# Moving the parts of an attention head by a slot in a hand-planned schedule

## The chip, the cores and the metric

The kernel runs on one core of a Trainium2 chip. The metric is the device time of one execution in microseconds (us), as a median over several executions; lower is better.

## The reference

Attention with a causal window of 128 and ALiBi slopes (4 batches, 8 heads, 576 positions, head size 64), and two layers that each multiply the 2304 rows by a 512x2048 and a 2048x512 matrix:

```python
scores = scale * np.matmul(q, k.transpose(0, 1, 3, 2))
mask = (rel >= 0) & (rel < 128)
scores = np.where(mask, scores + bias[None], -1000000000.0)
attn = np.exp(scores - np.max(scores, axis=-1, keepdims=True))
attn = attn / (np.sum(attn, axis=-1, keepdims=True) + 1e-09)
x = heads_side_by_side(np.matmul(attn, v))          # 2304 x 512
...
h = x @ w_in;  g = h * np.clip(h + 3.0, 0.0, 6.0) / 6.0;  x = g @ w_out     # first layer
h = x @ w_in;  g = s * np.maximum(h, 0.0) ** 2 + b;       x = g @ w_out     # second layer
```

## The kernel before

**Groups, heads, steps.** The rows are cut into eight groups of one batch each: four of 256 rows (two 128-row blocks), then four of 320 rows (three blocks, of which the last has 64 rows). Attention of group g makes the tile x of group g, in eight heads. The heads of groups 0 and 1 have a form of their own (class StartUnit). From group 2, "the third group", on they are of class Unit, 48 in all. The first layer goes through the groups, in 16 steps f for each: a step multiplies x by one 128-column piece of w_in (the twelve matmuls of h, L576), applies the activation, and multiplies by the piece of w_out (o, L634, twelve matmuls). A step's matmuls have 256 columns in groups 0 to 3 and 320 in groups 4 to 7. The second layer follows in tiles of 384 rows (L648). Each value is split into a rounded part ("hi") and a remainder ("lo"), so that every product is made of three matmuls.

**The order.** All instructions are written down by a planner: `at(slot, rank, fn)` puts a function into a slot, and the program is emitted slot by slot, by rank within one. Each engine executes its instructions in that order. Layer steps are two slots apart, heads four slots apart, so two steps stand beside each head; those whose f is even and odd are called the even and the odd step here. While group g's steps run, the heads of groups g+1 and g+2 are made.

**One step's chain.** h goes to PSUM, in one bank (tag "h", a single buffer) up to the last group. ScalarE (ACT) applies ReLU (L589), VectorE (DVE) multiplies (L593, called the product below) and so frees the bank: the next step's h waits for it. Then ACT rounds (L606) and DVE takes the remainder (L613); o of that step comes after the next step's h.

**One head's chain (Unit).**

- `load` (L277, L283): DMAs on the SP queue, into one of two buffers raw. A load waits until the head two before has been read by its remainders.
- `casts` (L291, L292, ACT): rounded q and k.
- `rests` (L296 on DVE, L301 on GpSimd, POOL): their remainders.
- `products` (L320, PE): scores of the first two blocks ("first products"), and a slot later of the third block ("second products"), which heads of groups 4 to 7 alone have. There are 32 of those heads.
- `minima` (L336, L337, DVE), `exps` (L347, ACT), `sums` (L354, L357, DVE), `weights` (L363, POOL: division by the sum).
- `transposes` (L372, PE), `fold` (L376, ACT: copy to F), `masks` (L388, POOL).
- every second head `values` (L403, PE), `to_hi` (L414, ACT) and `to_lo` (L418, DVE: remainder of x).

Up to about 140 us the weights of the first layer are still being prepared (class Half): a DMA (L168) on the same SP queue, two ACT instructions (L178, L179, tile z), two on DVE (L183, L186), one on POOL (L192), one on ACT (L200) and one on DVE (L204). This part of the time is called the weight stage.

Of the kernel before, what the change touches and what calls it, by code (L numbers as in the profile page):

```python
# [23 lines left out]
def tile_alibi_window_attention_moe_moe2(  # L24
# [45 lines left out]
    def at(slot, rank, fn):  # L70
        plan.setdefault(slot, []).append((rank, len(plan[slot]), fn))
# [70 lines left out]
    class Half:  # L142
# [10 lines left out]
        def plan(self, s):  # L153
            at(s - 3, 1, self.load)
            at(s, 30.1, self.high)
            at(s, 38, self.sign)
            at(s + 1, 31, self.add)
            at(s + 2, 31.2, self.hi)
            at(s + 3, 31, self.lo)
# [79 lines left out]
    class Unit:  # L239
# [10 lines left out]
        def plan(self, s):  # L250
            two = min(self.qa + 2, self.qb)
            at(s - 7, 1, self.load)
            at(s - 1, 34, self.casts)
            at(s + 1, 33, self.rests)
            at(s + 3, 20, lambda: self.products(self.qa, two))
            at(s + 4, 20, lambda: self.products(two, self.qb))
            at(s + 3, 32, lambda: self.minima(self.qa, two))
            at(s + 4, 32.7, lambda: self.minima(two, self.qb))
            at(s + 5, 33, lambda: self.exps(self.qa, two))
            at(s + 5, 33, lambda: self.exps(two, self.qb))  # L260
            at(s + 6, 32.2, self.sums)
            at(s + 7, 33, self.weights)
            at(s + 9, 20, self.transposes)
            at(s + 9, 35, self.fold)
            at(s + 10, 30.02, self.masks)
            if self.h % 2:
                at(s + 13, 20, self.values)
                at(s + 14, 39, self.to_hi)
                at(s + 15, 39, self.to_lo)

        def pair(self):
            return units[self.g * H + self.h // 2 * 2 :][:2]
# [444 lines left out]
    for f in range(NF):  # L717
        for i, s in enumerate((hslot[0, f], oslot[0, f])):
# [3 lines left out]
            s = min(s - 6, 3 + 4 * f + 2 * i)  # L722
# [3 lines left out]
    for k in range(2 * NF):  # L726
        f, i = divmod(k, 2)
        s = max(last + 6 + int(1.74 * k), oslot[nt1 - 1, f])
# [25 lines left out]
    with tc.manual_schedule():  # L754
        for slot in sorted(plan):
            for _, _, fn in sorted(plan[slot], key=lambda x: x[:2]):
                fn()
# [55 lines left out]
```

## Time and profile before

| | us |
|---|---|
| median of 3 executions (953.79 to 955.13) | 953.92 |
| the profiled execution | 956.32 |
| its span, first to last instruction | 954.5 |
| PE busy in the span | 930.8 |
| weight loads of PE (PEld) busy | 857.1 |
| DVE busy | 531.2 |
| ACT busy | 466.2 |
| POOL busy | 271.7 |

The profiled execution is one more execution, 2.4 us over the median; 1.8 us of its time lie outside the span. PE's matmuls and its weight loads are shown as two engines, PE and PEld. The granted clock of TensorE was 0.999 over the whole span.

### The profile page before, as it was taken

How to read it: one execution, taken by the hardware profiler on the slowest of the kernel's cores; microseconds unless marked ns; L12 is line 12 of the kernel's file. 1: busy time of each engine (PE TensorE's matmuls, PEld its weight loads, DVE VectorE, ACT ScalarE, POOL GpSimd, SP SyncE). 2: the span in 40 equal slices, each digit the busy share in tenths (PEclk: the TensorE clock that was granted, in tenths of full speed). 3: DMA queues.
4: the chain of work that ended last, by engine and by line, in shares of the span. 5: the costliest groups of instructions: out<-in, count | busy, mean ns of one | idle time of the engine just before them, and what ended most of it. 6: DMA issues, size and time to landing. Idle time of an engine off the chain costs nothing.

```text
span 954.5 us, 16386 instructions
## 1 busy us (share of the span) xinstructions
PE 930.8 (98%) x6014; PEld 857.1 (90%) x6017; DVE 531.2 (56%) x1334; ACT 466.2 (49%) x1201; POOL 271.7 (28%) x544
## 2 busy tenths in 40 slices
PE   8898999999999999999999999999999999999998
PEld 4587899999999999999999988899999999999997
DVE  6998885555555555555259999633323323323322
ACT  6987875455455454454248757523223223323322
POOL 6635763345544434443114433100000000000000
PEclk9999999999999999999999999999999999999999
DMA  8425533123131222220045355010200200200000
GB/s 319 147 70 177 172 112 99 58 89 96 61 95 61 71 75 62 73 78 13 1 158 192 133 183 163 25 41 1 67 1 1 67 1 1 67 1 1 34 1 33
DMA packets 34383, 73.92 MB, mean 77 GB/s; under 512 B 4352, under 2 KB 13568, under 8 KB 34304
## 3 DMA queue, kind: packets, MB, share of 16 engines
q1 hardware_dynamic: 34304, 72.89, 23.2%
q8 instruction: 47, 0.77, 0.3%
q14 instruction: 32, 0.26, 0.1%
HBM read 63.44 MB, written 9.44 MB: 76 GB/s over the span
## 4 chain that ended last, share of the span: by engine, by line
PE 75%; DVE 13%; ACT 4%; issue 3%; DMA 3%; POOL 1%; SPq 0%; POOLq 0%; ACTq 0%; DVEq 0%
PE h L576 34%; PE o L648 18%; PE o L634 16%; DVE w L204 3%; DVE z L183 3%; PE s L320 3%; PE v L403 3%; DMA raw<-w 2%; PE t L372 2%; DVE raw L186 1%; DVE t L597 1%; ACT z L178 1%; DVE g L613 1%; DVE g L615 1%; DVE t L593 1%
## 5 line engine op out<-in xcount | busy, mean ns | idle before, releaser
L576 PE MATMUL h<-x,w 128*128 128x384 f32 (+2 forms) x2688 | 444.9, 314 | 4.5 <-DVE t L593 3.9
L576 PEld LDWEIGHTS h<-x,w 128*128 128x128 f32 x2688 | 416.4, 189 | 15.6 <-DVE t L593 6.3
L589 ACT ACTIVATE t<-h 128x384 f32<-128x384 f32 (+2 forms) x224 | 99.5, 444 | 366.4 <-PE h L576 366.3
L634 PE MATMUL o<-g,w 128*128 128x256 f32 (+1 forms) x1536 | 230.4, 299 | 2.5 <-ACT g L606 1.2
L648 PE MATMUL o<-w,g 128*128 128x512 f32 x864 | 217.0, 395 | 3.4 <-ACT g L608 1.9
L634 PEld LDWEIGHTS o<-g,w 128*128 128x128 f32 x1536 | 210.0, 189 | 4.7 <-ACT g L606 2.0
L648 PEld LDWEIGHTS o<-w,g 128*128 128x128 f32 x864 | 159.9, 188 | 36.3 <-ACT g L608 4.4
L597 DVE SCALAR_TENSOR_TENSOR t<-t,s_sb 128x384 f32<-128x384 f32 x96 | 63.2, 658 | 171.5 <-ACT t L589 171.5
L388 POOL TENSOR_SCALAR_AFFINE_SELECT W<-F 128x128 f32<-128x128 f32 (+1 forms) x240 | 68.2, 322 | 150.1 <-ACT F L376 149.1
L593 DVE SCALAR_TENSOR_TENSOR t<-t,h 128x256 f32<-128x256 f32 (+1 forms) x128 | 57.6, 450 | 84.1 <-ACT t L589 84.1
L613 DVE TENSOR_TENSOR g<-t,g 128x256 fp32r<-128x256 f32 (+1 forms) x128 | 72.5, 566 | 40.9 <-ACT g L606 40.2
L615 DVE SCALAR_TENSOR_TENSOR g<-t,b_sb,g 128x384 fp32r<-128x384 f32 x96 | 63.6, 663 | 54.1 <-ACT g L608 54.0
L608 ACT ACTIVATE g<-t,b_sb 128x384 fp32r<-128x384 f32 x96 | 59.2, 617 | 63.6 <-DVE t L597 63.6
L192 POOL TENSOR_TENSOR raw<-raw 128x512 int32<-128x512 int32 x47 | 54.9, 1168 | 105.5 <-DVE raw L186 73.1
L606 ACT ACTIVATE g<-t 128x256 fp32r<-128x256 f32 (+1 forms) x128 | 55.9, 436 | 15.5 <-DVE t L593 15.4
L301 POOL TENSOR_TENSOR C<-raw,C 64x448 fp32r<-64x448 f32 (+1 forms) x48 | 51.0, 1063 | 36.2 <-issue 18.4
L363 POOL TENSOR_SCALAR P<-P,st 128x128 f32<-128x128 f32 x128 | 53.2, 431 | 7.1 <-DVE st L357 5.6
L347 ACT ACTIVATE P<-P,st 128x128 f32<-128x128 f32 x128 | 49.6, 391 | 0.0
L336 DVE COPY_PREDICATED s<-own,s 128x128 f32<-128x128 int32 (+1 forms) x112 | 30.8, 275 | 32.4 <-PE s L320 30.7
L183 DVE TENSOR_SCALAR z<-z 128x512 int32<-128x512 int32 x64 | 44.1, 689 | 3.3 <-ACT z L178 2.8
L337 DVE CUSTOM_DVE_ANT_0 P<-s,rel 128x128 f32<-128x128 f32 x128 | 37.1, 290 | 7.3
L204 DVE TENSOR_TENSOR w<-raw,w 128x512 fp32r<-128x512 f32 x47 | 41.2, 876 | 0.0
(73 smaller groups left out, 762.8 us busy)
## 6 DMA issues: line engine op xcount, KB each, us to landing
raw<-w SPq DMA_DIRECT2D x47, 512.0 KB, 4.3
raw<-qk SPq DMA_DIRECT2D x32, 384.0 KB, 3.1
stage<-w SPq DMA_DIRECT2D x17, 512.0 KB, 4.4
out<-y SPq DMA_DIRECT2D x18, 256.0 KB, 2.3
raw<-qk SPq DMA_DIRECT2D x16, 256.0 KB, 2.7
rv<-v SPq DMA_DIRECT2D x16, 256.0 KB, 3.4
raw<-qkv0p SPq DMA_DIRECT2D x8, 384.0 KB, 7.7
x2d<-y SPq DMA_DIRECT2D x8, 320.0 KB, 2.4
```

What stands on the lines that cost most here:

```text
L183: nc.vector.tensor_scalar(out=z, in0=z, scalar1=3, scalar2=None, op0=ALU.logical_shift_left)
L204: nc.vector.tensor_tensor(out=w[:, 1, self.c], in0=self.l.bitcast(F32), in1=w[:, 0, self.c].bitcast(F32), op=ALU.subtract,)
L388: nc.gpsimd.affine_select(out=self.W[:, o : o + r], in_=self.F[:, q : q + r], fill=0.0, base=k - 1, compare_op=ALU.is_ge, pattern=[[s, r]] ...
L576: nc.tensor.matmul(self.ps, lhsT=w[:, wp, cc * P : (cc + 1) * P], rhs=x[:, cc, xp], start=m == 0, stop=m == 3 * CC - 1,)
L589: nc.scalar.activation(self.a, self.ps, AF.Relu, **bias)
L593: nc.vector.scalar_tensor_tensor(out=self.a, in0=self.a, scalar=6.0, in1=self.ps, op0=ALU.min, op1=ALU.mult)
L597: nc.vector.scalar_tensor_tensor(out=self.a, in0=self.a, scalar=s_sb, in1=self.a, op0=ALU.mult, op1=ALU.mult)
L608: nc.scalar.activation(self.g[:, 0], self.a, AF.Identity, bias=b_sb)
L613: nc.vector.tensor_tensor(out=self.g[:, 1], in0=self.a, in1=hi, op=ALU.subtract)
L615: nc.vector.scalar_tensor_tensor(out=self.g[:, 1], in0=self.a, scalar=b_sb, in1=hi, op0=ALU.add, op1=ALU.subtract,)
L634: nc.tensor.matmul(acc[t][d], lhsT=w[:, wp, DM + d * P : DM + (d + 1) * P], rhs=self.g[:, gp], start=f == 0 and i == 0 and (t > 1 or d % 2 ...
L648: nc.tensor.matmul(acc[t][tb], lhsT=self.g[:, gp, tb * P : (tb + 1) * P], rhs=w[:, wp, DM:], start=f == 0 and i == 0, stop=f == NF - 1 and ...
```

## The change

Seven of the numbers that place a head's parts are changed: casts, remainders and division move one slot ahead; transposes, copy, masks, values and the two stores of x one slot back. Loads, products, minima, exponentials and sums stay.

```diff
@@ class Unit, plan @@
             at(s - 7, 1, self.load)
-            at(s - 1, 34, self.casts)
-            at(s + 1, 33, self.rests)
+            at(s - 2, 34, self.casts)
+            at(s, 33, self.rests)
...
-            at(s + 7, 33, self.weights)
-            at(s + 9, 20, self.transposes)
-            at(s + 9, 35, self.fold)
-            at(s + 10, 30.02, self.masks)
+            at(s + 6, 33, self.weights)
+            at(s + 10, 20, self.transposes)
+            at(s + 10, 35, self.fold)
+            at(s + 11, 30.02, self.masks)
             if self.h % 2:
-                at(s + 13, 20, self.values)
-                at(s + 14, 39, self.to_hi)
-                at(s + 15, 39, self.to_lo)
+                at(s + 14, 20, self.values)
+                at(s + 15, 39, self.to_hi)
+                at(s + 16, 39, self.to_lo)
```

What it does to the order is shown at one place that repeats: steps 6 and 7 of group 3, with heads 4 to 7 of group 4 (names s0_2_6 and qY0_102<-raw0_2_7 are the scores of its head 6 and the remainder of q of its head 7; t3_6 and h3_6 are the activation and h of step 6).

On DVE, from the second minima of head 6 to the sums, before:

```order
L336 COPY_PREDICATED s0_2_6_4_3508<-own_90,s0_2_6_4_3508 128x64
L337 ISA P0_2_6_3470,st0_2_6_3471<-s0_2_6_4_3508,rel_91 128x128
L337 ISA st0_2_6_3471 128x1
L593 SCALAR_TENSOR_TENSOR t3_6_3522<-t3_6_3522,h3_6_3495 128x256
L296 SCALAR_TENSOR_TENSOR qY0_102<-raw0_2_7_3291,qX0_98 128x320
L613 TENSOR_TENSOR g3_6_3564<-t3_6_3522,g3_6_3564 128x256
```

and of the change:

```order
L336 COPY_PREDICATED s0_2_6_4_3507<-own_90,s0_2_6_4_3507 128x64
L337 ISA P0_2_6_3475,st0_2_6_3476<-s0_2_6_4_3507,rel_91 128x128
L337 ISA st0_2_6_3476 128x1
L296 SCALAR_TENSOR_TENSOR qY0_102<-raw0_2_7_3293,qX0_98 128x320
L418 TENSOR_TENSOR x4_3251<-v0_2_3_3434,x4_3251 128x320
L593 SCALAR_TENSOR_TENSOR t3_6_3520<-t3_6_3520,h3_6_3494 128x256
L613 TENSOR_TENSOR g3_6_3555<-t3_6_3520,g3_6_3555 128x256
```

The remainder of q, which stood behind step 6's product L593, now stands ahead of it, and so does, at every second head, the remainder of x (L418), which stood two slots further up, ahead of an L613.

On PE, from h of step 6 to the first products of head 7, before (the left out rows are the twelve of o):

```order
L576 MATMUL h3_6_3495<-x3_2383,w1_6_886 128x256 x12
L320 MATMUL s0_2_6_4_3508<-C0_2_6_3361,qX1_99 128x192
L320 MATMUL s0_2_6_4_3508<-C0_2_6_3361,qY1_103 128x192
L372 MATMUL t0_2_5_3518<-ident_89,P0_2_5_3352 128x128 x3
...
L576 MATMUL h3_7_3544<-x3_2383,w1_7_976 128x256 x12
L320 MATMUL s0_2_7_2_3569<-C0_2_7_3479,qX0_98 128x256
```

and of the change:

```order
L576 MATMUL h3_6_3494<-x3_2401,w1_6_886 128x256 x12
L320 MATMUL s0_2_6_4_3507<-C0_2_6_3338,qX1_99 128x192
L320 MATMUL s0_2_6_4_3507<-C0_2_6_3338,qY1_103 128x192
...
L576 MATMUL h3_7_3538<-x3_2401,w1_7_976 128x256 x12
L372 MATMUL t0_2_5_3551<-ident_89,P0_2_5_3358 128x128 x3
L320 MATMUL s0_2_7_2_3568<-C0_2_7_3455,qX0_98 128x256
```

The transposes (and values, where there are any) have moved from between h of the even step and h of the odd step to behind h of the odd step.

On ACT, from the ReLU of step 6 to that of step 7, before:

```order
L589 ACTIVATE t3_6_3522<-h3_6_3495 128x256
L347 ACTIVATE P0_2_6_3470,st0_2_6_3471<-P0_2_6_3470,st0_2_6_3471 128x128 x3
L376 ACTIVATE F0_2_5_3530<-t0_2_5_3518 128x320
L606 ACTIVATE g3_6_3564<-t3_6_3522 128x256
L589 ACTIVATE t3_7_3574<-h3_7_3544 128x256
L291 ACTIVATE qX1_99<-raw1_2_0_3397 128x320
```

and of the change:

```order
L589 ACTIVATE t3_6_3520<-h3_6_3494 128x256
L347 ACTIVATE P0_2_6_3475,st0_2_6_3476<-P0_2_6_3475,st0_2_6_3476 128x128 x3
L606 ACTIVATE g3_6_3555<-t3_6_3520 128x256
L291 ACTIVATE qX1_99<-raw1_2_0_3399 128x320
L292 ACTIVATE C1_2_0_3563<-raw1_2_0_3399 128x448
L376 ACTIVATE F0_2_5_3566<-t0_2_5_3551 128x320
L589 ACTIVATE t3_7_3580<-h3_7_3538 128x256
```

Casts and copy F have come to stand ahead of the odd step's ReLU.

## Rows read from the trace of the kernel before

**Rows 1.** Windows: busy time (and instructions) by stage; clock, DMA share, GB/s.

```profile
core 0: us, PE busy (x) PEld busy (x) DVE busy (x) ACT busy (x) POOL busy (x), PEclk, DMA share, GB/s
60.00:140.00 80.00, 72.72 (x568) 66.93 (x568) 71.71 (x175) 64.26 (x163) 50.38 (x68) 1.00 0.42 137
140.00:475.00 335.00, 335.00 (x2649) 327.12 (x2648) 179.01 (x646) 162.17 (x543) 142.46 (x370) 1.00 0.21 66
```

**Rows 2.** Waits of PE's weight loads, 60 to 140 us: total, times, longest.

```profile
PEld h L576 <- DVE t L593: 5.5, 9, 1.4
```

**Rows 3.** Who waited for the score matmuls L320, whole span: us, times.

```profile
  DVE s L336: 30.7, 32
```

**Rows 4.** Timeline of PE's weight loads at a 256-column step: start, us, what.

```profile
240.27 0.19 PEld L320 LDWEIGHTS s<-C,qX 128*128 128x128 f32 x1
...
240.52 0.32 PEld L372 LDWEIGHTS t<-ident,P 128*128 128x128 f32 x3
240.81 1.50 PEld L634 LDWEIGHTS o<-g,w 128*128 128x128 f32 x12
242.23 0.43 PEld L576 LDWEIGHTS h<-x,w 128*128 128x128 f32 x3
```

**Rows 5.** Timeline of DVE at the same step.

```profile
240.79 0.23 DVE L336 COPY_PREDICATED s<-own,s 128x64 f32<-128x64 int32 x1 [0.61 <-PE s L320]
...
241.27 0.42 DVE L593 SCALAR_TENSOR_TENSOR t<-t,h 128x256 f32<-128x256 f32 x1
241.60 0.48 DVE L296 SCALAR_TENSOR_TENSOR qY<-raw,qX 128x320 fp32r<-128x320 f32 x1
```

**Rows 6.** Timeline of PE's weight loads at a 320-column step.

```profile
303.67 0.19 PEld L320 LDWEIGHTS s<-C,qX 128*128 128x128 f32 x1
...
303.94 0.32 PEld L372 LDWEIGHTS t<-ident,P 128*128 128x128 f32 x3
304.23 1.76 PEld L634 LDWEIGHTS o<-g,w 128*128 128x128 f32 x12
305.95 0.19 PEld L576 LDWEIGHTS h<-x,w 128*128 128x128 f32 x1
```

**Rows 7.** Timeline of DVE at that step.

```profile
304.21 0.23 DVE L336 COPY_PREDICATED s<-own,s 128x64 f32<-128x64 int32 x1 [1.05 <-PE s L320]
...
304.69 0.48 DVE L593 SCALAR_TENSOR_TENSOR t<-t,h 128x320 f32<-128x320 f32 x1
305.09 0.49 DVE L296 SCALAR_TENSOR_TENSOR qY<-raw,qX 128x320 fp32r<-128x320 f32 x1
```

**Rows 8.** Timeline of DVE at a remainder of x.

```profile
239.36 0.49 DVE L418 TENSOR_TENSOR x<-v,x 128x320 fp32r<-128x320 f32 x1
239.76 0.41 DVE L613 TENSOR_TENSOR g<-t,g 128x256 fp32r<-128x256 f32 x1
```

**Rows 9.** Timeline of PE's weight loads where h waits, in the weight stage.

```profile
64.23 1.51 PEld L576 LDWEIGHTS h<-x,w 128*128 128x128 f32 x12
65.67 1.51 PEld L634 LDWEIGHTS o<-g,w 128*128 128x128 f32 x12
67.59 0.30 PEld L576 LDWEIGHTS h<-x,w 128*128 128x128 f32 x2 [0.40 <-DVE t L593]
```

**Rows 10.** The product on DVE that it waited for.

```profile
67.12 0.41 DVE L593 SCALAR_TENSOR_TENSOR t<-t,h 128x256 f32<-128x256 f32 x1
```

**Rows 11.** Timeline of ACT: a ReLU, and a copy F.

```profile
240.64 0.38 ACT L589 ACTIVATE t<-h 128x256 f32<-128x256 f32 x1 [1.84 <-PE h L576]
...
249.26 0.44 ACT L376 ACTIVATE F<-t 128x320 f32<-128x320 f32 x1 [0.33 <-PE t L372]
```

**Rows 12.** Timeline of POOL and DVE: remainder of k, and an L613 beside it.

```profile
245.42 1.16 POOL L301 TENSOR_TENSOR C<-raw,C 64x448 fp32r<-64x448 f32 x1
...
246.12 0.74 DVE L613 TENSOR_TENSOR g<-t,g 128x256 fp32r<-128x256 f32 x1
```

**Rows 13.** Waits of the SP queue, 56 to 145 us: total, times, longest.

```profile
SPq L277 <- DVE qY L296: 70.9, 10, 17.1
```

**Rows 14.** Timeline of ACT: a weight piece that has not landed.

```profile
126.80 0.65 ACT L178 ACTIVATE z<-raw 128x512 f32<-128x512 f32 x1 [0.87 <-DMA raw<-w]
```

**Rows 15.** Waits of DVE, 60 to 140 us: total, times, longest.

```profile
DVE z L183 <- ACT z L178: 2.8, 4, 1.0
```

**Rows 16.** Line L296, all instructions: duration in ns, least, median, greatest.

```profile
L296 DVE SCALAR_TENSOR_TENSOR qY<-raw,qX x48: 409/484/835, 70.8 to 444.7; 128x320 fp32r<-128x320 f32 x32, 128x256 fp32r<-128x256 f32 x16
```

## The prediction

> **What bounds the kernel now.** I read the windows by stage first, then PE's waits, then the timelines of single steps. From 140 to 475 us PE is busy for the whole 335 us [rows 1]: in this stretch nothing but the number of matmuls sets the time, and no other engine is busy for more than 179 us. It holds most of the 48 moved heads, and a move can save nothing there; it can only bring a wait where there is none. In the weight stage, 60 to 140 us, PE is busy for 72.7 of 80 us and DVE for 71.7 [rows 1]. There PE waits above all for the product that frees the bank of h [rows 2]. All that the change may win is there, all that it may lose is after it.
>
> **What the change does from 140 us on: the even step.** DVE waits for the second products before the second minima, at all 32 heads that have them [rows 3]. So that piece of DVE's queue is tied to PE: minima start right behind the score matmuls, then comes the product, and the next h waits for it. The change puts the remainder of q, and at every second head the remainder of x, between the two, and takes the transposes (and values) out of PE's stretch up to that h. DVE's part gets longer and PE's shorter.
>
> A 256-column step, counted from the first load of the second products (240.27 [rows 4]). PE: three transpose loads take 240.52 to 240.81, 0.29; without them o's loads start at 0.25, and h's 1.42 later (240.81 to 242.23), at 1.67. DVE: the product starts at 1.00 (241.27 [rows 5]) and takes 0.42. A 320-wide instruction of the remainder's kind takes its engine 0.40 up to the next one (304.69 to 305.09 [rows 7]), the remainder of x as much (239.36 to 239.76 [rows 8]). With the remainder of q ahead the product ends at 1.82, with both at 2.22. From a product's end to the waiting load were 0.06 us (67.12 + 0.41 to 67.59 [rows 9, 10]), so h's loads start at 1.88 or 2.28: **0.21 or 0.61 late**. That such a wait counts in full is seen in the same rows: from o to h 1.92 instead of 1.44.
>
> A 320-column step, from 303.67 [rows 6]: o at 0.27, h 1.72 later, at 1.99. The product now starts at 1.02 and takes 0.48 [rows 7]; it ends at 1.90 or 2.30, and h is released at 1.96 or 2.36: **0 or 0.37 late**, the first with 0.03 to spare.
>
> How many of each: a head's second products stand 16 slots and 4 for each later head of its group ahead of its group's first step. So heads 0 to 7 of group 4 and 0 to 2 of group 5 have 256-column steps beside them, 11; the other 21 have 320. The remainder of x of an odd head falls three heads later, on heads with an even number: 6 of the 11 and 10 of the 21. Sum: 6 x 0.61 + 5 x 0.21 + 10 x 0.37 + 11 x 0 = **8.4 us**. Bounds: with the full durations, 0.49 in place of 0.40 for each instruction, 0.30, 0.79, 0.06 and 0.55, or 12.4. If one weight load could be made while h waits (1.42/12 or 1.72/12, 0.12 or 0.14 at each of 21 late steps), 5.7. I take 8.4, since rows 9 show the first load of a waiting h not made ahead. The Trainium skill ("TensorE: Matmul & The Clock Gate", the section on the array's architecture) says that PE's queue can pull weight loads ahead of matmuls in flight. By that rule the sum would be near 5.7; the load at 67.59 started only with its release, and the trace decides.
>
> **The odd step.** Its ReLU now stands behind copy F, which waits for the transposes behind h. Until the next h PE has these (0.29), the first products and o (1.42 or more), over 1.71 us; the chain is transposes 0.29, F 0.44, ReLU 0.38 [rows 11], product 0.42, so 1.53. The first products' four loads are the margin; it costs nothing. With that cover gone it would be a few tenths at 32 heads.
>
> L613 of the odd step also comes later by about F's 0.44, and may then run beside POOL's remainder of k, which follows the masks now. In such a meeting it took 0.74 instead of 0.41 [rows 8, 12]. Idle ahead of the second minima were 0.61 (256) and 1.05 (320) [rows 5, 7]; 0.44 + 0.33 is over the former by 0.16. For the 11 heads that is 0 to 1.8; I take half, **0.9**.
>
> Heads without second products (groups 2 and 3, up to about 195 us): remainders stand on DVE in time that is idle, as the product waits for h alone; nothing. Division a slot earlier and transposes a slot later: more slack, and PE did not wait there; nothing. The loads' waits move with the remainders; nothing here, since a load has most of two heads' time to land.
>
> **The weight stage.** Loads of q and k wait on the SP queue for the remainder of the head two before, 70.9 us in ten waits [rows 13]. The weight pieces' DMAs stand behind them on that queue, and a piece was late for ACT by 0.87 [rows 14]. With the remainders a slot ahead these DMAs start earlier. What hangs on it is DVE's wait for z: 2.8 us in four waits [rows 15]. On the other side, F and casts now delay the odd step's ReLU by up to 0.44 at some seven heads, 3.1 at most. The greatest gain is all of DVE's idle time, 80 - 71.7 = 8.3. I take the wait for z, **-2.8**, which is nearest to the cause, and keep +3.1 to -8.3.
>
> **Sum.** 8.4 + 0.9 - 2.8 = 6.5. The profiled execution took 956.32 (span 954.5 and 1.8 around it), so 962.8 for it; the median lies 2.4 lower: 953.92 + 6.5 = **960.4 us**. No change can be told from one within 0.2%, or 1.9 us, here.
>
> **The rivals.** (1) *The weight stage gives more than the steps lose.* If the late pieces were what all engines of that stage hang on, the whole 8.3 comes back, and the steps cost their lower bound, 5.7: 951.3. For it speaks that all ten waits end with the remainder; against it that DVE is 90% busy there and that its own order isn't shortened. It decides from a gain over the steps' loss: a weight stage shorter by 8 us. (2) *They cancel*: a gain of 7 to 8 against 8.4, 953 to 955.5, no difference. (3) *Remainders meet on the shared side.* Both remainders of a head now stand in one slot. If they run at the same time, DVE's takes its longest, 835 ns instead of 484 [rows 16]: 0.35 more at 32 heads, 11 us, so 971. Against it: POOL must first do the masks, which wait for F, while DVE waits for the second products, later. The Trainium skill ("SBUF — State Buffer", the section on two separate sides) says that DVE with two SBUF inputs and a GpSimd instruction that reads SBUF lock each other out for a whole instruction; by that rule a remainder that comes second waits for up to all of the other. Rows 12 agree: L613 ends 0.28 after POOL's instruction.
>
> **How the numbers follow.** My forecast, a wait of h at even steps beside a small gain in the weight stage: 0.70, with 956 to 966 of its own. Rival 3 0.08, rival 2 0.12, rival 1 0.10. The range of 8 in 10 takes in rival 2 and the forecast up to its upper bound: 954 to 967. Slower by over 0.2%: 0.78; the same: 0.12; faster: 0.10.
>
> **What would show it.** In the profile after: waits of h L576 for the product L593 from 195 to 455 us, some 20, of 0.2 to 0.6 us each, longer at even-numbered heads and in groups 4 and 5; PE busy time in that stretch short of the whole by their sum; in the weight stage fewer waits of z for DMAs and an earlier end. It is wrong if h doesn't wait there, that is, if second minima start earlier or h's loads later than in rows 4 to 7; or if the weight stage ends over 6 us earlier.

## The result, and the profile after

The changed kernel takes **965.48 us** (median of 4 executions, 965.12 to 965.51), the kernel before 954.26 (4 executions): ratio 1.0116, 95% interval 1.0098 to 1.0133. It is 11.2 us slower. The execution profiled after took 965.46, its span 963.7. The execution profiled before took 956.32, which is 2.4 over the median; a second trace of the same kernel ("before, second trace" below: 954.33 us, span 952.5) shows that 2.0 of it are a longer weight stage in that one execution, and that from about 130 us on the two run alike.

The first part of the page after: busy time, share and instructions of each engine.

```profile
PE 935.6 (97%) x6014; PEld 857.3 (89%) x6017; DVE 542.9 (56%) x1334; ACT 471.0 (49%) x1201; POOL 255.7 (27%) x544
```

Against the first trace PE is busy 4.8 us longer and DVE 11.7, and POOL 16 less, with the same number of instructions. The windows say in which stretch (PE, PEld, DVE, ACT, POOL; then the clock, the share of the DMAs, GB/s). After:

```profile
60.00:140.00 80.00, 70.37 (x564) 66.37 (x564) 77.44 (x172) 64.34 (x163) 41.96 (x67) 1.00 0.42 137
140.00:480.00 340.00, 337.37 (x2617) 323.92 (x2616) 183.54 (x645) 165.62 (x540) 134.88 (x371) 1.00 0.21 65
```

Before, second trace:

```profile
60.00:140.00 80.00, 74.05 (x585) 68.75 (x584) 73.35 (x177) 65.08 (x167) 51.80 (x68) 1.00 0.45 137
140.00:480.00 340.00, 340.00 (x2680) 332.12 (x2679) 179.15 (x647) 163.22 (x544) 141.98 (x369) 1.00 0.21 65
```

Two things: in the weight stage PE does 21 matmuls fewer in the same 80 us and DVE is busy 4.1 us longer; and after it, where PE was busy for the whole stretch [rows 1], 63 matmuls fewer fit. PE's busy time falls by 2.6 there, the weight loads' by 8.2. So the loss is read from PEld or from the starts of instructions: most of it doesn't show as idle time of PE.

What the loads wait for after the weight stage (140 to 480 us: total, times, longest). Before, no wait of h was there at all. (These lists leave out idle times under 0.15 us. A step that is 0.2 late leaves less than that, so it is not in them.)

```profile
PEld h L576 <- DVE t L593: 6.7, 17, 0.5
...
PEld v L403 <- issue: 2.1, 11, 0.2
```

One of these steps, 256 columns, with both remainders ahead of the product; PE's weight loads:

```profile
243.00 0.19 PEld L320 LDWEIGHTS s<-C,qX 128*128 128x128 f32 x1
243.12 0.19 PEld L320 LDWEIGHTS s<-C,qY 128*128 128x128 f32 x1
243.23 1.50 PEld L634 LDWEIGHTS o<-g,w 128*128 128x128 f32 x12
245.26 1.49 PEld L576 LDWEIGHTS h<-x,w 128*128 128x128 f32 x12 [0.54 <-DVE t L593]
```

and DVE (with POOL's remainder of k, which runs beside the first row):

```profile
242.06 1.15 POOL L301 TENSOR_TENSOR C<-raw,C 64x448 fp32r<-64x448 f32 x1
...
242.45 1.04 DVE L613 TENSOR_TENSOR g<-t,g 128x256 fp32r<-128x256 f32 x1
243.51 0.23 DVE L336 COPY_PREDICATED s<-own,s 128x64 f32<-128x64 int32 x1
...
244.00 0.49 DVE L296 SCALAR_TENSOR_TENSOR qY<-raw,qX 128x320 fp32r<-128x320 f32 x1
244.40 0.48 DVE L418 TENSOR_TENSOR x<-v,x 128x320 fp32r<-128x320 f32 x1
244.80 0.41 DVE L593 SCALAR_TENSOR_TENSOR t<-t,h 128x256 f32<-128x256 f32 x1
```

Against [rows 4, 5]: o's loads follow the second products at once; the product starts 1.80 us after the first of these loads instead of 1.00; h's loads 2.26 after it instead of 1.96. The prediction had 2.28. A 320-column step with both remainders, PE's weight loads:

```profile
309.28 0.19 PEld L320 LDWEIGHTS s<-C,qX 128*128 128x128 f32 x1
...
309.54 1.77 PEld L634 LDWEIGHTS o<-g,w 128*128 128x128 f32 x12
311.64 1.02 PEld L576 LDWEIGHTS h<-x,w 128*128 128x128 f32 x7 [0.34 <-DVE t L593]
```

Against [rows 6]: 2.36 from the first load to h, which is what the prediction had, instead of 2.28.

The waits in the weight stage (60 to 140 us), after:

```profile
PE s L320 <- ACT F L376: 3.0, 2, 1.5
...
PEld h L576 <- DVE t L593: 8.9, 11, 1.2
...
PEld s L320 <- POOL P L363: 3.3, 2, 1.7
```

and before, second trace:

```profile
PEld h L576 <- DVE t L593: 5.9, 9, 1.7
...
PEld t L372 <- POOL P L363: 3.0, 8, 0.6
```

h waits for the product longer than before [rows 2]. The transposes no longer wait for the division, but two first products now wait, 1.5 us each. Of the two names that the profile gives for that wait, the first products use nothing of POOL's division L363; so I take it to be copy F, which ends at 106.05 in the rows below, just before the first product starts. ACT and then PE, after:

```profile
103.94 0.65 ACT L178 ACTIVATE z<-raw 128x512 f32<-128x512 f32 x1 [0.62 <-DVE raw L186]
104.52 0.66 ACT L179 ACTIVATE raw<-raw 128x512 int32<-128x512 uint32 x1
105.08 0.40 ACT L291 ACTIVATE qX<-raw 128x256 fp32r<-128x256 f32 x1
105.39 0.40 ACT L292 ACTIVATE C<-raw 128x256 fp32r<-128x256 f32 x1
105.69 0.36 ACT L376 ACTIVATE F<-t 128x256 f32<-128x256 f32 x1
...
106.20 0.30 PE L320 MATMUL s<-C,qX 128*128 128x128 f32 x1 [1.51 <-ACT F L376]
```

F reads the transposes' bank, and the first products need a bank. F now stands behind a weight piece, which waited for DVE, and behind two casts. DVE and POOL just before:

```profile
104.14 1.04 POOL L192 TENSOR_TENSOR raw<-raw 128x512 int32<-128x512 int32 x1 [3.11 <-DVE raw L186]
...
104.16 1.04 DVE L354 TENSOR_SCALAR st<-st 128x2 f32<-128x2 f32 x1
```

The sum L354 works on two columns. It takes 1.04 us here, from within 0.02 us of POOL's start to 0.02 after its end. The groups of these lines (busy, mean ns), 60 to 140 us, after:

```profile
L613 DVE TENSOR_TENSOR g<-t,g 128x256 fp32r<-128x256 f32 x20 | 13.2, 662 | 0.1
...
L354 DVE TENSOR_SCALAR st<-st 128x2 f32<-128x2 f32 x8 | 7.4, 926 | 0.0
...
L363 POOL TENSOR_SCALAR P<-P,st 128x128 f32<-128x128 f32 x16 | 5.8, 376 | 2.8 <-DVE st L357 2.0 <-ACT C L292 0.8
```

and before, second trace:

```profile
L363 POOL TENSOR_SCALAR P<-P,st 128x128 f32<-128x128 f32 x16 | 13.3, 843 | 0.0
...
L613 DVE TENSOR_TENSOR g<-t,g 128x256 fp32r<-128x256 f32 x21 | 10.5, 499 | 2.7 <-ACT g L606 2.7
...
L354 DVE TENSOR_SCALAR st<-st 128x2 f32<-128x2 f32 x8 | 2.8, 354 | 0.0
```

In total POOL's division is 7.5 us shorter and DVE's two lines are 7.3 longer. Which instructions ran side by side stands in the timelines. In the second trace the division starts 0.03 us behind a weight piece's remainder on DVE, L204, and its two instructions take 1.93 us (after: 0.73):

```profile
99.39 0.69 DVE L204 TENSOR_TENSOR w<-stage,w 128x512 fp32r<-128x512 f32 x1
...
99.42 1.93 POOL L363 TENSOR_SCALAR P<-P,st 128x128 f32<-128x128 f32 x2
```

After, it is L613 that runs beside POOL's remainder of k, at eight of its twenty places (three of 21 in the second trace), and the sum that runs beside the addition L192, at seven of eight (one of eight):

```profile
99.96 1.07 POOL L301 TENSOR_TENSOR C<-raw,C 64x256 fp32r<-64x256 f32 x1
...
100.35 0.96 DVE L613 TENSOR_TENSOR g<-t,g 128x256 fp32r<-128x256 f32 x1
```

That 7.5 and 7.3 are one time, moved from POOL to DVE, is not shown: the experiments below have longer remainders L613 without a shorter division (e6), and a shorter division without longer sums (e8).

**Where the 11.2 us are.** The first matmul of a head's second products marks each of the 32 heads (16 to 47, groups 4 to 7). Starts in us, read from timelines of PE; the last columns are how much later than before:

```
head   before   after    later, by head     since head 16
16     196.24   196.68
20     225.48   227.41
21     232.24   234.77   0.60 (from 20)     2.09
22     240.38   243.11   0.20               2.29
27     277.27   282.19                      4.48
28     286.36   291.59   0.31               4.79
29     294.39   299.98   0.36               5.15
30     303.81   309.43   0.03               5.18
47     451.41   460.62   0.36 (from 46)     8.77
```

8.8 us are lost step by step from head 16 on. What is left is the weight stage: from its end to head 15 the changed kernel stays 2.4 us behind the second trace of before. 8.8 + 2.4 = 11.2. The 8.8 can be read to the tenth; the 2.4 stands on one trace of each kernel, and two traces of the kernel before differ by 2.0 in this stage, so it is luck that the sum fits so closely.

The 0.31 at head 28 is a late step beside head 27, where group 4's first 320-column step meets the last o of 256 columns. PE's weight loads, after:

```profile
282.05 0.19 PEld L320 LDWEIGHTS s<-C,qX 128*128 128x128 f32 x1
...
282.30 1.49 PEld L634 LDWEIGHTS o<-g,w 128*128 128x128 f32 x12
284.01 1.76 PEld L576 LDWEIGHTS h<-x,w 128*128 128x128 f32 x12 [0.22 <-DVE t L593]
```

With the prediction's own numbers: o of 256 columns would let h's loads start at 0.25 + 1.42 = 1.67, the product of 320 columns behind one remainder releases them at 1.96, 0.29 late. The trace has 1.96.

### The profile page after: what moved, and what is told of

It is laid out like the page before. It is cut to its first block, busy times and chain, and to the rows that moved or that the text cites. A ratio compares the mean times of both kernels' runs of the same rounds, so it can differ in the third digit from the quotient of the medians.

```text
span 963.7 us, 16432 instructions
## 1 busy us (share of the span) xinstructions
PE 935.6 (97%) x6014; PEld 857.3 (89%) x6017; DVE 542.9 (56%) x1334; ACT 471.0 (49%) x1201; POOL 255.7 (27%) x544
## 4 chain that ended last, share of the span: by engine, by line
PE 73%; DVE 19%; ACT 4%; issue 3%; DMA 1%; SPq 0%; ACTq 0%; DVEq 0%
PE h L576 35%; PE o L648 18%; PE o L634 13%; DVE z L183 3%; DVE w L204 3%; PE s L320 3%; PE v L403 3%; DVE raw L186 2%; DVE t L593 2%; PE t L372 2%; DVE g L613 1%; DVE t L597 1%; ACT z L178 1%; DVE qY L296 1%; DVE x L418 1%
## 5 line engine op out<-in xcount | busy, mean ns | idle before, releaser
L634 PE MATMUL o<-g,w 128*128 128x256 f32 (+1 forms) x1536 | 227.2, 297 | 1.6 <-DVE g L613 1.2
L593 DVE SCALAR_TENSOR_TENSOR t<-t,h 128x256 f32<-128x256 f32 (+1 forms) x128 | 57.4, 449 | 120.6 <-ACT t L589 120.6
L613 DVE TENSOR_TENSOR g<-t,g 128x256 fp32r<-128x256 f32 (+1 forms) x128 | 85.1, 665 | 28.4 <-ACT g L606 27.2
L363 POOL TENSOR_SCALAR P<-P,st 128x128 f32<-128x128 f32 x128 | 45.9, 376 | 157.8 <-ACT C L292 122.5
L192 POOL TENSOR_TENSOR raw<-raw 128x512 int32<-128x512 int32 x47 | 55.2, 1175 | 117.5 <-DVE raw L186 50.5
L388 POOL TENSOR_SCALAR_AFFINE_SELECT W<-F 128x128 f32<-128x128 f32 (+1 forms) x240 | 57.8, 282 | 42.5 <-ACT F L376 42.4
L376 ACT ACTIVATE F<-t 128x320 f32<-128x320 f32 (+1 forms) x48 | 20.0, 417 | 67.0 <-PE t L372 60.5
L204 DVE TENSOR_TENSOR w<-raw,w 128x512 fp32r<-128x512 f32 x47 | 40.5, 862 | 0.0
```

Of the source, the lines that this page charges most:

```text
L204: nc.vector.tensor_tensor(out=w[:, 1, self.c], in0=self.l.bitcast(F32), in1=w[:, 0, self.c].bitcast(F32), op=ALU.subtract,)
L388: nc.gpsimd.affine_select(out=self.W[:, o : o + r], in_=self.F[:, q : q + r], fill=0.0, base=k - 1, compare_op=ALU.is_ge, pattern=[[s, r]] ...
L593: nc.vector.scalar_tensor_tensor(out=self.a, in0=self.a, scalar=6.0, in1=self.ps, op0=ALU.min, op1=ALU.mult)
L613: nc.vector.tensor_tensor(out=self.g[:, 1], in0=self.a, in1=hi, op=ALU.subtract)
L634: nc.tensor.matmul(acc[t][d], lhsT=w[:, wp, DM + d * P : DM + (d + 1) * P], rhs=self.g[:, gp], start=f == 0 and i == 0 and (t > 1 or d % 2 ...
```

## The experiments

All ran beside the kernel before, in three batches (e0 to e3, e4 to e7, e8 to e11) in which it took 955.15, 955.46 and 954.81 us. First the kernel before again, for its trace.

> The kernel before, unchanged, for a second trace of it. The change cost 11.2 us between medians but only 9.2 between the two profiled spans (954.5 and 963.7), since the profiled execution of before was 2.4 over its median. If the weight stage's length varies from execution to execution, this span is near 952.5 and the first products of group 3's last head come some 2 us earlier than 185.5; if the 2 us lie elsewhere, they come at 185.5 as in the first trace.

954.33 us; the trace is the "second trace" above. The weight stage of the kernel before differs by 2 us between executions, so one trace alone can't price anything in it.

**The product first (e1).** The change, but in groups 4 to 7 both remainders behind the product:

```diff
+            m = 1 if self.qa else 0
-            at(s, 33, self.rests)
+            at(s + m, 33, self.rests)
-                at(s + 16, 39, self.to_lo)
+                at(s + 16 + m, 33.1 if m else 39, self.to_lo)
```

> The changed kernel, but for heads of groups 4 to 7 the remainder of q and the remainder of x stand behind the even step's product on DVE (a slot later than in the change). Theory: the even steps' waits are made by these two instructions alone; 8.8 us come back, 956.7, and no wait of h for the product is left after 195 us. Rival (copy F ahead of the odd step's ReLU, or PE's new order, makes them): nothing comes back, 965.5.

958.09 us, ratio 1.0030 (1.0019 to 1.0041). From head 16 to 47 the second products fall behind by 1.0 instead of 8.8, and the list of waits has none of h after 140 us. So these two places in DVE's order carry 7.8 of the 11.2. Of the 1.0 that is left, 0.3 is lost by head 19: 0.13 at heads 17 and 19, where the remainder of x belongs to group 3 and still stands ahead of the product. From head 28 on it is 0.02 to 0.04 at every head. One wait is there once in the kernel before and twelve times here:

```profile
PEld v L404 <- issue: 2.3, 12, 0.2
```

But the loss is as large at heads without values, and ahead of the values PE has a gap of 0.09 us in the second trace too. What PE's timeline shows at every such head is the first products behind the transposes: from their start to o it takes 0.55 us (308.31 to 308.86) where it took 0.47 in the second trace (305.85 to 306.32). The other o, which no longer stands behind the transposes, wins 0.06 of it back (1.78 instead of 1.84 from its start to h).

**The two halves in groups 4 to 7 (e2, e3).** The kernel before, with the forward moves alone, and with the backward moves alone (here m is 1 in groups 4 to 7, else 0):

```diff
-            at(s - 1, 34, self.casts)          # e2
-            at(s + 1, 33, self.rests)
-            at(s + 7, 33, self.weights)
+            at(s - 1 - m, 34, self.casts)
+            at(s + 1 - m, 33, self.rests)
+            at(s + 7 - m, 33, self.weights)
-            at(s + 9, 20, self.transposes)     # e3: so for all six
+            at(s + 9 + m, 20, self.transposes)
```

> The kernel before, with the forward moves alone (casts, remainders, division), for groups 4 to 7. Theory: the remainder of q delays the product by 0.40, but the transposes (0.29, and values 1.2 at each second head) are still in PE's stretch up to the next h: the product then releases h at 1.88 against 1.96 (256 columns), 1.96 against 2.28 (320); no wait, 954.3, the same. Rival: the remainder's place alone costs, 11 x 0.2 to 32 x 0.4, 956.5 to 967.

> The kernel before, with the backward moves alone (transposes, copy, masks, values, stores of x), for groups 4 to 7. Theory: with the remainder of q behind the product again, only the remainder of x stands ahead of it, at each second head: 0.2 late at 6 narrow heads, nothing at wide ones; 955.5, so the two halves cost 0 and 1.2 and together 8.8. Rival: PE's shorter stretch or copy F is what costs: 960 or more.

955.71, ratio 1.0006 (0.9997 to 1.0016), and 956.67, ratio 1.0015 (1.0005 to 1.0024). In the trace of e2 the second products of heads 16 to 47 lose 0.00 together, in e3 1.5: 0.18 to 0.19 at each of four heads with 256 columns and a remainder of x, about 0.03 at most others. So the halves cost 0 and 1.5 there, and together 8.8. The prediction's sum has the reason: with the remainder of q alone the product releases h at 1.88, and with the transposes in their old place h's loads start at 1.96 anyway. With the backward half alone the remainder of x alone stands ahead, 0.21 late by the sum. Each half leaves most of the slack that the other one uses up.

**One remainder of the two (e9).** As e1, but only the remainder of x goes behind the product, and the remainder of q stays ahead.

> The change, but in groups 4 to 7 the remainder of x behind the product; the remainder of q stays ahead of it. Theory, each instruction ahead of the product counts by itself: 6 x 0.40 + 10 x 0.37 = 6.1 of the 11.2 us come back, 959.4 us, and the starts of the second products still fall behind by 0.2 at each head with a 256-column step and by next to nothing at the others. Rival, one instruction ahead of the product is enough for the late release: 963 or more.

960.73 us, ratio 1.0066 (1.0052 to 1.0080): 5.9 us over the kernel before, so 5.3 of the 11.2 are back. The second products fall behind by 0.18 to 0.21 at each head from 20 to 27, whether even or odd, by 0.30 at head 28, and by 0.03 from 29 on; at heads 17 and 19, whose remainder of x belongs to group 3 and stayed ahead, still by 0.54. The waits of h, 140 to 480 us:

```profile
PEld h L577 <- DVE t L594: 1.2, 3, 0.5
```

They stand beside heads 16, 18 and 27. Each instruction counts by itself: the remainder of x 0.40 at 256 columns (0.60 against 0.20), and 0.34 at 320 (0.37 against 0.03), where the first 0.03 had been to spare. The expectation had 6.1 come back, because it counted all sixteen late heads; with the two of group 3 left out it is 6.1 - 0.8 = 5.3 (by the starts in the traces 5.0).

**The weight stage (e4 to e8, e11).** Moves in groups 2 and 3 alone (m is 1 there, else 0): all of them (e4), the forward half (e5), the backward half (e6), casts and remainders alone (e7), the division alone (e8), and e4 with copy F ahead of the casts on ACT (e11):

```diff
-            at(s + 9 + m, 35, self.fold)
+            at(s + 9 + m, 33.5 if m else 35, self.fold)
```

> The kernel before, with all the moves for the heads of groups 2 and 3 alone (the weight stage and some 50 us behind it). Theory: the weight stage loses by itself what the trace after shows against an undisturbed trace of before, 2.4 us, and nothing follows; +2.4. Rival (the stage gains, as forecast, and what the trace shows comes from elsewhere): -2.8.

> The kernel before, with the forward moves alone (casts, remainders, division) for groups 2 and 3. Theory: the weight pieces start earlier (DVE's wait for z, 1.0 us in the undisturbed trace, goes), but POOL's remainder now meets L613 on DVE (+2.7 in the trace after); PE's waits for copy F (3.0) don't arise, since the transposes stay: between -1 and +1. Rival: all the loss of the stage hangs on the forward moves: +2.4.

> The kernel before, with the backward moves alone (transposes, copy F, masks, values, stores of x) for groups 2 and 3. Theory: these make the first products wait for a PSUM buffer that copy F frees late (two waits, 3.0 us in the trace after), and they take the masks from ahead of POOL's addition L192, which then meets the sums L354 on DVE (354 to 926 ns each): +2 to +3. Rival: no loss without the forward moves, within 0.5.

> The kernel before, with casts and remainders alone a slot ahead for groups 2 and 3, division in its old place. Theory: as the run with all forward moves but for the division, which had waited for DVE at its old place (843 against 376 ns); between -1.5 and +0.5. Rival: the division's move is what helps, and without it the stage is as before, within 0.3.

> The kernel before with one of the five moves, in groups 2 and 3 alone: the division a slot ahead. Theory, the division's move is what the forward half of these groups gains by, since POOL's division no longer holds up the transposes (3.0 us of PE's waits in the kernel before): 953.8 us, as with the whole forward half, and no wait of t for P. Rival, it gains only together with the remainders: 955 to 956, as the kernel before.

> All moves in groups 2 and 3 alone, as in an earlier run (957.2 us), but with copy F ahead of the casts on ACT and not behind them; DVE's order is the same. Theory, the first products' two waits of 1.5 us for the bank that F empties are what the weight stage loses: they go, and the time falls by 2 to 3 us, to 954.2 to 955.2. Rival, the loss is DVE's: its sums and additions still run beside POOL's, so 957 stays.

| moves in groups 2 and 3 | us | ratio (95%) | L354, L613, L363: mean ns, 60 to 140 us | PE waiting for F |
|---|---|---|---|---|
| none (e0) | 954.33 | | 354, 499, 843 | 0.3 |
| all (e4) | 957.22 | 1.0018 (1.0009 to 1.0028) | 1034, 650, 372 | 3.0 |
| forward (e5) | 953.80 | 0.9981 (0.9972 to 0.9990) | 540, 611, 368 | none |
| backward (e6) | 956.69 | 1.0010 (1.0001 to 1.0020) | 479, 660, 895 | 0.4 |
| casts, remainders (e7) | 955.56 | 0.9999 (0.9990 to 1.0008) | 355, 522, 827 | 0.3 |
| division (e8) | 955.51 | 1.0003 (0.9995 to 1.0012) | 336, 658, 371 | 1.5 |
| all, F first (e11) | 957.64 | 1.0030 (1.0018 to 1.0041) | 823, 655, 373 | 0.9 |

The moves of these 16 heads cost 1.8 us with all of them, so the stage has the sign that the prediction's term had not. The forward half gains 1.7, the backward half loses 1.2; as after the weight stage, the two together are not their sum. For the backward half the expected wait for F did not come about (0.4 instead of 3.0), and its profiled execution, 958.01, was the longest of its ten, so its row tells little of the median. Neither part of the forward half gains by itself: e7 gave nothing, as its rival said, which put the gain on the division; and the division alone (e8) gave nothing either. The gain needs both. In e11 the waits for F shrank, and counted from the first head its weight stage is 1.0 us shorter than e4's in the traces, but 0.8 is lost again at heads 13 to 15, and the time isn't lower. So the two long waits for F are not the whole loss. What remains open is how the loss divides between F's lateness and POOL's additions beside DVE's sums (the sums are longest where the loss is largest, e4 and e11, but not in e6). The columns of means and waits come from one trace each. h's longer waits for the product don't tell: e5, which gains, has 9.1 us of them, more than any. An experiment that shifts only the sums away from POOL's addition was not tried.

**The forward half everywhere (e10).**

```diff
-            at(s - 1, 34, self.casts)
-            at(s + 1, 33, self.rests)
-            at(s + 7, 33, self.weights)
+            at(s - 2, 34, self.casts)
+            at(s, 33, self.rests)
+            at(s + 6, 33, self.weights)
```

> The forward moves (casts and remainders, division) for groups 2 to 7, the backward ones for none. Theory, what they gave alone adds up, -1.7 in groups 2 and 3 and 0 in 4 to 7: 953.8 us, faster than both kernels. Rival, in groups 4 to 7 the remainders cost something once the weight stage no longer covers it: 956 or more.

953.57 us (11 executions) beside 954.81, ratio 0.9985 (0.9977 to 0.9994). This and e5 are the only versions faster than both kernels, by 1.5 and 1.9 thousandths; the second products of heads 16 to 47 lose 0.02 together. Its weight stage, the window and three waits:

```profile
60.00:140.00 80.00, 73.86 (x593) 69.78 (x593) 76.97 (x179) 66.10 (x170) 44.17 (x68) 1.00 0.43 138
```

```profile
PEld h L576 <- DVE t L593: 8.8, 13, 1.2
...
ACT z L178 <- DMA stage<-w: 0.2, 1, 0.2
...
ACT z L178 <- DMA raw<-w: 0.2, 1, 0.2
```

593 matmuls in the 80 us instead of 585 [rows 1 have 568], with the same longer waits of h, but no wait of the transposes for the division, none for F, and 0.4 for late weight pieces where the second trace has 3.0.

## Why the prediction was right, and where not

- **The sign and the range were right**, 965.5 in 954 to 967. The value, 960.4, was 5 us low, nearly all of it one term.
- **Even step: right in mechanism, in place and in size.** Predicted late by 0.61, 0.21, 0.37 and 0; the heads fall behind by 0.54 to 0.60, 0.20, 0.36 to 0.40 and 0.03, and one by 0.31. Sum 8.4, measured 8.8. The runs agree with the sum's parts: each remainder's 0.40 (e9), the remainder of x alone (e3), and the cover of 0.08 that lets the forward half alone cost nothing (e2). The total is a little nearer than its terms. Head 27 was counted among the 21 with 320 columns, at nothing, but its o still has 256: 0.3 too little. The other odd heads with 320 columns lose 0.03 each, 0.3 in all, where the sum had nothing; this stays in e1 and comes with the backward half (e3) and not with the forward half (e2). And the heads with 0.61 lose 0.2 less together, above all the first two, whose remainder of x has 256 columns and not 320.
- **The rule on pulled-ahead loads.** If one load were made while h waits, the sum would have been 5.7, and the late steps 0.12 or 0.14 shorter each. They were not. In each of the seventeen waits of h the first load starts 0.05 us after the product's end. The Trainium skill ("TensorE: Matmul & The Clock Gate", the section on the array's architecture) lets the queue pull weight loads ahead of matmuls in flight; here the first load of a matmul that waits for its bank comes with the release and not before, as 245.26 shows, against the product's end at 245.21.
- **Odd step: 0.9 for L613 was too much.** The meeting is there, and larger than thought: 1.04 us instead of 0.74. But L613 ends at 243.49, and the second minima start 0.51 after the first load of their products; in [rows 4, 5] it was 0.52. The whole margin of 0.61 is used and nothing is lost, so 0. That the ReLU behind F costs nothing after the weight stage agrees: no wait of an odd step's h is left in e1.
- **Groups 2 and 3 after the weight stage: nothing, right.** From head 8 to 15 the distance to the second trace stays at 2.4.
- **Weight stage: wrong, -2.8 predicted, +2.4 by the traces and +1.8 by e4.** The step that failed is "I take the wait for z, -2.8, which is nearest to the cause". The cause came about: DVE's wait for z [rows 15] is gone. But its 2.8 us were read from an execution with a long weight stage; the second trace has 1.0. And freed idle time is a gain only if it isn't used up: the prediction took DVE's busy time as given. In the trace after, DVE is busy for 77.4 of 80 us instead of 71.7 (73.4 in the second trace), with three to five instructions fewer. POOL runs beside DVE in other pairs: L613 and L354 are 7.3 us longer than in the second trace, L613 beside the remainder of k, L354 beside the addition L192. How much of the loss is theirs and how much is F's stays open. The prediction looked for such meetings after the weight stage and not in it. It did hold the two ingredients, +3.1 for F and casts ahead of the ReLU as a bound, and rival 3 for meetings; F's lateness struck first products and not the ReLU alone.
- **Rivals.** (1) and (2) needed a gain in the weight stage of 7 us or more; the best that any run there gave is 1.7. (3) did not come about for the remainders of q: over all 48 the longest is 0.489 us, shorter than the 0.835 of [rows 16]. That both remainders "now" stand in one slot was misread: one function writes both, before the change too. The meetings came, with other instructions.
- **What would show it.** Seventeen waits of h of 0.22 to 0.54 us, where some 20 of 0.2 to 0.6 were expected, at every second head and head 27 (the steps that are 0.2 late are too short for the list): as written. The weight pieces' waits for DMAs went too, from 4.9 us in the first trace and 3.0 in the second to none in the list. "PE busy time short of the whole by their sum" was not: it is short by 2.6 of 6.7, and PEld shows the rest. The weight stage doesn't end earlier.
- **The base.** The median of before was 953.92 in the first three executions and 954.8 to 955.5 in the three batches; the ratio is the safer number.

## What to carry to other kernels

Where one engine's short instructions release the one that bounds, count what stands between the event that starts them and the release, and what the bounding engine has to do meanwhile: the difference of the two, step by step, gave the loss to 0.4 in 8.8 us. Two moves that cost little each (0 and 1.5 us here) can cost much together (8.8), when each lives on slack that the other takes; so price a change as a whole, and try its halves one by one, since one half may be a gain that the other hides. And idle time that a move frees on a nearly full engine is not yet a gain: look for what its instructions will now run beside.

## What the hardware showed that was not expected

- An operation of DVE on 128x2 elements took 1.01 to 1.05 us, instead of 0.15 to 0.26, when it ran beside a POOL addition of two 128x512 tiles that had started 0.02 to 0.33 us earlier: seven of the eight sums in the weight stage after, one of eight in the second trace. It ended 0.02 to 0.03 us after POOL's. The eighth sum started just as close behind POOL's addition, and there the addition was longer, 1.08 instead of 1.04, and the sum was not:

```profile
137.72 1.08 POOL L192 TENSOR_TENSOR raw<-raw 128x512 int32<-128x512 int32 x1 [3.12 <-ACT C L292]
...
137.74 0.16 DVE L354 TENSOR_SCALAR st<-st 128x2 f32<-128x2 f32 x1
```

In the traces of e1 and e11 three and two of eight sums went that way. So at a distance of 0.02 us a meeting can go either way. That this is why the weight stage's length differs between executions is possible and not shown.
- The Trainium skill ("SBUF — State Buffer", the section on two separate sides) says that DVE, in a mode that uses both ports or with two inputs in SBUF, and a GpSimd instruction lock each other out for the whole instruction. For L613, with two inputs, the trace agrees (1.04 instead of 0.41); the sum has one tensor input, and no run here shows which mode it uses, only that it is held for just as long.
- In the meetings shown with more than 0.02 us between the starts, the cost lay with the one that came second: L613, 0.39 us behind the remainder of k, took 0.96 instead of 0.42; the two instructions of the division, the first 0.03 behind L204, took 1.93 instead of 0.73. With the division alone a slot ahead (e8) POOL's mean for it fell from 843 to 371 ns and the mean of DVE's remainder L613 rose from 499 to 658. The transposes' waits for the division (3.0 us in the second trace) are gone there, and still the time is not lower: 955.51 beside 954.81.
